# A planned order refitted: 60 zero matmuls first, zeros in every early wait, another load rate in the planner's model, and the last batch's rows stored whole

## The chip, the cores and the metric

The kernel runs on one core of a Trainium2 chip. Its time is the device time in microseconds (us) of one execution; a kernel's time is the median of several executions. The profile is of one further execution. A core has five engines that matter here: TensorE (PE, matmuls, with weight loads shown as PEld), VectorE (DVE), ScalarE (ACT), GpSimd (POOL, which issues the loads) and SyncE (SP, which issues the stores). Each engine runs its instructions strictly in the order in which the program lists them.

## The reference

Attention over 8 batches, 12 heads, 448 tokens and 64 dimensions per head, and then a feed-forward stage on the joined heads. The inputs are float32.

```python
scores = (1 / sqrt(64)) * q @ k^T                 # q, k, v: (8, 12, 448, 64)
attn   = softmax(scores);  x = attn @ v           # -> x: (3584, 768)
h      = x @ w_in                                 # w_in: (768, 2048)
g      = h * sigmoid(h)
out    = g @ w_out                                # w_out: (2048, 768) -> (3584, 768)
```

The draw has scores small enough that the kernel takes no maximum before the exp.

## The kernel before

**Units.** Heads are worked on in groups of four (`HG = 4`, so `NG = 3` groups in a batch). A unit is one group of one batch; batch 0's groups are each cut into two units of 224 queries (`PIECES`), so that there are six units for batch 0 and 21 for the others, 27 in all.

**Loads.** Keys, queries, values and both weights are loaded by POOL's queue, each cast to float16 on the way: `load_k` (tile `rk`, two buffers), `load_q` (`rq`, three), `load_v` (`V`, two), `load_w_in`, `load_w_out`. The order of the loads is written out by hand (`plan_k(0, hg)` and so on, around line 685): batch 0's keys, queries and values, then quarters of `w_in` with more queries between, batch 1's first keys, the rest of `w_in`, the first half of `w_out`, batch 1's values, the second half of `w_out`, and then batch after batch. A token of batch 0's `(i g)` layout is spread so that partition `i` of a head holds 14 tokens in a row; because of this, 32 rows of an output tile lie 14 rows apart in the output.

**Attention.** DVE turns keys and queries (`turn_k` to `KT`, `turn_q` to `QT`, lines 293 and 304). PE makes scores in bursts of one quarter of the keys (`scores`, tile `s`, line 319: two PSUM buffers of two banks), ACT takes the exp (`expo`, `E`, line 356), DVE adds up pairs of exp tiles (`add_e`, `T`, line 367), and PE makes, for each unit, the sums (part 0, with `ones`) and the two halves of the weighted values (parts 1 and 2): `attend`, tile `a`, line 383. DVE turns the sums (`sT`, line 423), inverts them (`inv`, 429), spreads them again (`rdn`, 432) and scales the values (`norm`, tile `xT`, line 440). From the second key group of batch 1 on, two units share one burst and their sums are made together.

**Feed-forward.** `ffn1` (`h`, line 454) is six matmuls for each of 16 blocks of 128 columns, followed by ACT's tanh (`th`, 465) and DVE's gate (`G` or `X`, 501). The second product is done for the first two row tiles plainly (`plain`, `o`, line 559), and for all others as quads of row tiles with seven products in place of eight (`product`, `p`, line 545); for these DVE first makes sums of the weights (`combine_w`, `D1`, `D4`, `D6` and two in `w_out_t`, line 491) and of the gated tiles (`combine_g`, `S`, line 535). Results go through ACT or DVE into `ost` and are stored by `store`, 32 rows in each DMA.

**PSUM.** `h`, `a`, `p`, `o` and the zeros' tile `z` share tag `m`: four banks in turn. So a new tile waits until the fourth one before it has been read.

**What sets the order.** Nothing is scheduled by the framework: `tc.manual_schedule` takes all engines. A planner in the kernel (`Order`, `Op`, `Ring`) runs a clock over a model of the engines at build time, with a cost for each operation (`mm`, `act`, and numbers in the `Op` calls), a rate for the loads (`DMA_RATE`, MB per us, and `DMA_TAIL`), and rings that stand for buffers. On ACT and DVE it picks, among the operations that are ready in the model, the one with the smallest ready time plus bias. On PE a burst of scores is run when it is ready and `PACE` has passed since the last, attention next, feed-forward otherwise (the loop at line 1162). The instructions are then emitted by the model's clock. On the chip the engines keep this order, whatever the real times are.

**Zeros.** Until the first `ffn1`, the planner fills a wait of PE with matmuls of a tile of zeros into `z` (`run_zeros`, line 1153):

```python
if warm["on"] and od.free["PE"] <= od.now and wait > 0.1 and od.now > 1.0:
    n = max(1, int((wait - 0.06) / mm(128)))
```

The softmax here doesn't subtract the row's maximum and nothing guards it: scores larger than these inputs give would overflow.

## Time and profile before

| | |
|---|---|
| median of five runs | 403.54 us |
| the five runs | 402.67, 403.46, 403.54, 408.07, 408.41 us |
| the profiled execution, its own time | 402.61 us |
| its span, first to last instruction | 400.8 us |
| TensorE clock granted, mean | 1.00 |
| busy: PE, DVE, ACT, POOL | 392.2, 301.2, 234.1, 88.7 us |
| loaded by POOL's queue | 22.82 MB written, in 27712 packets |
| zero matmuls | 102, 73 of them before the first score |

A line of the timeline reads: start in us from the span's start, length, engine, line of the kernel, operation, tile written <- tiles read with their shapes, number of instructions merged, and in brackets how long the engine stood idle before it and what ended that. Matmuls overlap, so that one matmul's length is more than its place in the queue; what a block costs is the distance from its first start to the next block's.

### The profile page before, as it was taken

What the parts mean: (1) busy time and instruction counts of PE and PEld (TensorE: products, weight loads), DVE (VectorE), ACT (ScalarE), POOL (GpSimd) and SP (SyncE); (2) the same over time, 40 slices, a digit from 0 to 9 for tenths busy, and PEclk for the clock granted to TensorE, in tenths of its full rate; (3) what the DMA queues carried; (4) which work ended last, traced back from release to release, by engine and by line L of the source; (5) the groups of instructions that cost most, each with busy time, mean ns of one, the idle gap of its engine ahead of it and who ended that gap; (6) DMA issues with size and microseconds to landing.
All of it is one profiled execution on the core that took longest, in us unless ns stands there. A gap on an engine that the chain in (4) does not pass through costs nothing.

```text
span 400.8 us, 9398 instructions
## 1 busy us (share of the span) xinstructions
PE 392.2 (98%) x3758; PEld 201.4 (50%) x3758; DVE 301.2 (75%) x646; ACT 234.1 (58%) x360; POOL 88.7 (22%) x160
## 2 busy tenths in 40 slices
PE   8999999999999999999999999999999999999995
PEld 7676754444444444444445444444345555555562
DVE  2566667999997987998776976986985765775763
ACT  3887886696856768467367529747776124123410
POOL 7743565623006350400170114300000000000000
PEclk9999999999999999999999999999999999999999
DMA  8999999947027942641192527411001220122014
GB/s 120 193 203 206 160 168 203 168 60 116 2 56 116 195 58 37 110 86 46 40 147 46 104 68 93 69 41 41 2 0 42 65 54 2 40 71 50 2 40 118
DMA packets 38507, 34.43 MB, mean 86 GB/s; under 512 B 11712, under 2 KB 37696, under 8 KB 38464
## 3 DMA queue, kind: packets, MB, share of 16 engines
q0 software_dynamic: 27712, 22.82, 38.9%
q1 hardware_dynamic: 10368, 10.63, 10.5%
q8 instruction: 29, 0.48, 0.5%
q10 hardware_dynamic: 384, 0.39, 0.4%
q14 instruction: 14, 0.11, 0.1%
HBM read 45.61 MB, written 11.01 MB: 141 GB/s over the span
## 4 chain that ended last, share of the span: by engine, by line
PE 95%; DVE 2%; ACT 1%; issue 1%; DVEq 0%
PE h L454 37%; PE p L545 30%; PE s L319 12%; PE a L383 12%; PE o L559 3%; PE z L1157 2%; ACT E L356 1%; DVE T L367 1%; DVE G L535 0%; DVE xT L440 0%; DVE ost L598 0%; ACT th L465 0%; DVE sT L423 0%; DVE rdn L432 0%; DVE inv L429 0%
## 5 line engine op out<-in xcount | busy, mean ns | idle before, releaser
L356 ACT ACTIVATE E<-s 128x896 f16<-128x896 f32 (+1 forms) x172 | 149.2, 915 | 46.5 <-PE s L319 45.4
L454 PE MATMUL h<-xT,w_in_t 128*128 128x448 f16 (+1 forms) x864 | 156.5, 332 | 0.2 <-DVE xT L440 0.2
L454 PEld LDWEIGHTS <-w_in_t 128*128 128x128 f16 x864 | 79.9, 98 | 70.5 <-issue 16.4
L465 ACT ACTIVATE th<-h 128x448 f16<-128x448 f32 (+1 forms) x144 | 71.6, 505 | 68.3 <-PE h L454 62.6
L501 DVE SCALAR_TENSOR_TENSOR G<-th,h 128x448 f16<-128x448 f16 (+2 forms) x144 | 75.2, 532 | 37.0 <-ACT th L465 35.5
L256 POOL DMA_DIRECT2D V<-in_v_dram x88 | 48.7, 570 | 102.6 <-PE a L383 86.0
L319 PE MATMUL s<-QT,KT 32*128 32x448 f16 (+4 forms) x864 | 54.9, 340 | 1.2 <-ACT E L356 1.2
L545 PEld LDWEIGHTS <-G 128*128 128x128 f16 x384 | 36.4, 98 | 29.1 <-issue 5.5
L545 PEld LDWEIGHTS <-S 128*128 128x128 f16 x312 | 29.1, 98 | 23.8 <-issue 5.8
L383 PE MATMUL a<-E,V 128*32 128x448 f16 (+3 forms) x864 | 40.5, 334 | 0.1
L545 PE MATMUL p<-D,G 128*128 128x384 f16 x208 | 38.0, 327 | 0.4 <-DVE xT L440 0.4
L545 PE MATMUL p<-w_out_t,S 128*128 128x384 f16 x208 | 37.0, 327 | 0.0
L440 DVE SCALAR_TENSOR_TENSOR xT<-a,rdn 128x448 f16<-128x448 f32 (+1 forms) x54 | 28.9, 562 | 8.4 <-PE a L383 7.5
L545 PE MATMUL p<-w_out_t,G 128*128 128x384 f16 x176 | 31.8, 326 | 0.0
L367 DVE TENSOR_TENSOR T<-T,E 128x1792 f16<-128x1792 f16 x20 | 21.8, 1088 | 12.8 <-ACT E L356 12.7
L319 PEld LDWEIGHTS <-KT 32*128 32x128 f16 (+2 forms) x864 | 16.4, 98 | 28.2 <-issue 27.2
L383 PEld LDWEIGHTS <-V 128*32 128x32 f16 (+2 forms) x864 | 18.4, 95 | 23.0 <-issue 15.1
L367 DVE TENSOR_TENSOR T<-E,E 128x1792 f16<-128x1792 f16 x20 | 21.7, 1083 | 6.1 <-ACT E L356 6.0
L535 DVE TENSOR_TENSOR S<-G 128x512 f16<-128x512 f16 x70 | 25.1, 415 | 0.7 <-PE p L545 0.7
L237 POOL DMA_DIRECT2D rk<-in_k_dram x24 | 13.7, 569 | 53.0 <-DVE KT L293 46.2
L293 DVE STREAM_TRANSPOSE KT<-rk 128x256 f32<-128x256 f32 (+3 forms) x48 | 16.6, 383 | 7.5 <-DMA rk<-in_k_dram 7.0
L423 DVE STREAM_TRANSPOSE sT<-a 128x448 f32<-128x448 f32 (+1 forms) x27 | 15.8, 585 | 4.7 <-PE a L383 4.3
(41 smaller groups left out, 251.1 us busy)
## 6 DMA issues: line engine op xcount, KB each, us to landing
out_dram<-ost SPq DMA_DIRECT2D x216, 48.0 KB, 1.6
rk<-in_k_dram POOLq DMA_DIRECT2D x24, 224.0 KB, 5.1
rq<-in_q_dram POOLq DMA_DIRECT2D x21, 224.0 KB, 5.7
w_out_t<-in_moe_w_out_dram POOLq DMA_DIRECT2D x8, 384.0 KB, 12.1
V<-in_v_dram POOLq DMA_DIRECT2D x43, 64.0 KB, 4.4
V<-in_v_dram POOLq DMA_DIRECT2D x40, 48.0 KB, 4.0
w_in_t<-in_moe_w_in_dram POOLq DMA_DIRECT2D x6, 256.0 KB, 7.2
w_in_t<-in_moe_w_in_dram POOLq DMA_DIRECT2D x3, 512.0 KB, 13.7
```

Of the source, the lines that this page charges most:

```text
L256: nc.gpsimd.dma_start(out=VT[b].rearrange("p h c i e -> p h c (i e)")[32 * x : 32 * (x + 1), hs, 0:count], in_=v[b, hs].rearrange("h (i g) ...
L293: nc.vector.transpose(out=turned.rearrange("p c x i -> p x c i")[:, x:y, 0:count], in_=t[:, first : first + count * (y - x)].rearrange("p ...
L319: nc.tensor.matmul(out=pS[p0 : p0 + 32 * (x1 - x0), h % 2, at : at + nq], lhsT=KT[(b, hg)][32 * h : 32 * (h + 1), c, x0:x1, :, e], rhs=QT[ ...
L356: nc.scalar.activation(out=E[(n, w)][0:kr, 2 * y : 2 * y + 2, 0:nk], in_=pS_t[(n, w, y)][0:kr, :, 0:nk], func=AF.Exp, scale=attn_scale,)
L367: nc.vector.tensor_tensor(out=T_t[n], in0=E[(n, 0)] if c == 1 else T_t[n], in1=E[(n, c)], op=ALU.add,)
L383: nc.tensor.matmul(out=a[32 * h : 32 * (h + 1), 0:nq], lhsT=w, rhs=e[k0:k1, h, at : at + nq], start=start, stop=stop,)
L440: nc.vector.scalar_tensor_tensor(out=xT[(b, cc)][:, 32 * g0 : 32 * g1], in0=acc[(n, part)][:, 0:nq], scalar=0.5, in1=rdn_t[n].rearrange("p ...
L454: nc.tensor.matmul(out=h[:, 0 : t1 - t0], lhsT=w_in_t[:, cc, 128 * f : 128 * (f + 1)], rhs=xT[(b, cc)][:, t0:t1], start=(cc == 0), stop=(c ...
L465: nc.scalar.activation(out=th, in_=h_t[(b, f, t0)][:, 0 : t1 - t0], func=AF.Tanh)
L501: nc.vector.scalar_tensor_tensor(out=dst[:, f, at + lo : at + hi], in0=th_t[(b, f, t0)][:, lo - t0 : hi - t0], scalar=1.0, in1=h_t[(b, f, ...
L535: nc.vector.tensor_tensor(out=dst[:, f0:f1], in0=x[:, f0:f1], in1=y[:, f0:f1], op=op)
L545: nc.tensor.matmul(out=pr_t[(qd, BANK[m])][:, 0:OH], lhsT=w[:, f, :], rhs=W_[m][:, f, :], start=(f == 0 and BANK[m] == m), stop=(f == HF - 1),
```

## The change

1. The planner's model: `DMA_RATE` from 0.37 to 0.405, with the loads of batch 0 counted a little heavier (1.3 and 1.25) and later keys and queries lighter (1.05 in place of 1.2); an exp's fixed cost from 0.093 to 0.052, copies' to 0.18, tanh's to 0.085; DVE's through a new `dve(n)` and 0.06 more until its result is seen; biases of tanh, gate, copies and sums; `PACE` from 3.4 to 4.2. None of these issues an instruction: they move the order of PE, ACT and DVE. The order of POOL's loads is as before.
2. Zeros: 60 at the start whatever the model says, and then in every wait over 0.05, with more of them for the same wait. The built program has 117 zero matmuls where 102 were, 62 of them before the first score.
3. Unit 0's keys are turned in two halves with its queries between, and its first scores need the first half alone.
4. Batch 7's queries are loaded head by head in another layout (four DMAs for a unit in place of one), by which 32 output rows in a row lie in 32 partitions; its results are stored with up to 128 rows in one DMA, and the last two tiles with one DMA on SP and one on ACT.
5. While batch 0's attention runs, scores that are ready go ahead of further attention parts, and an attention part goes ahead of feed-forward only when it has been ready for 0.5.

```diff
-DMA_RATE = 0.37
+DMA_RATE = 0.405
...
-def act(n):
-    return n * 0.000833 + 0.093
+def act(n, fixed=0.052):
+    return n * 0.000833 + fixed
+
+def dve(n):
+    return n / 960.0 + 0.07
...
+        if eng == "DVE":
+            tail += 0.06
...
-    PACE = 3.4
+    PACE = 4.2
...
+        if b == B - 1:
+            for h in range(HG):
+                nc.gpsimd.dma_start(
+                    out=t[32 * h : 32 * (h + 1)],
+                    in_=q[b, HG * hg + h].rearrange("(g i) d -> i g d", i=32),
+                )
+        else:
+            nc.gpsimd.dma_start(out=t, in_=group_of(q, b, hg)[:, D * g0 : D * g1])
...
-    def turn_k(b, hg):
+    def turn_k(b, hg, c0=0, c1=NCH):
...
+        last = 4 * qd + 4 == NT * B
+        w = 0
+        while w < 4:
             r, col = divmod(128 * t + 32 * w, S)
-            b = 2 * u + r
+            b, n = 2 * u + r, 1
+            cols = slice(OH * j, OH * (j + 1))
+            if b == B - 1:
+                n = 2 if last and i == j else 4 - w
+                dst = out[b * S + col : b * S + col + 32 * n, cols]
...
+            (nc.scalar if last and w else nc.sync).dma_start(
+                out=dst, in_=ost_t[(qd, i, j)][32 * w : 32 * (w + n), :]
             )
+            w += n
...
-        ld_k[(b, hg)] = od.load(1.2 * MB * TPP, lambda: load_k(b, hg), ring)
+        ld_k[(b, hg)] = od.load((1.05, 1.3)[b == 0] * MB * TPP, lambda: load_k(b, hg), ring)
...
-            mb = MB * (hg1 - hg0) * X_TOK[form(b, hg0)][x][1]
+            mb = MB * (hg1 - hg0) * X_TOK[form(b, hg0)][x][1] * (1.25 if b == 0 else 1)
...
+            if n == 0:
+                op.busy, op.emit = 0.42, lambda: turn_k(b, hg, 0, 2)
...
+        if n == 0:
+            more = Op("DVE", 0.4, lambda: turn_k(b, hg, 2, 4), [qt_op[n]], 20)
...
+    FIRST_ZEROS = 60
+    od.now = od.free["PE"]
+    od.on_pe(Op("PE", 5.0, lambda: run_zeros(FIRST_ZEROS)), "full")
+    od.now = 0.0
...
+                    if av_seq[0][0][0] < 6 and (x := qk_at()) is not None and x <= od.now + 0:
+                        break
...
-                if av is not None and av <= od.now - 0:
+                if av is not None and av <= od.now - 0.5:
...
-        if warm["on"] and od.free["PE"] <= od.now and wait > 0.1 and od.now > 1.0:
-            n = max(1, int((wait - 0.06) / mm(128)))
+        if warm["on"] and od.free["PE"] <= od.now and wait > 0.05 and od.now > 1.0:
+            n = max(1, int((wait - -0.06) / mm(128)))
```

## The prediction

> **What bounds the kernel now.** I read the page first: busy times, then the chain that ended last.

> ```profile
> span 400.8 us, 9398 instructions
> PE 392.2 (98%) x3758; PEld 201.4 (50%) x3758; DVE 301.2 (75%) x646; ACT 234.1 (58%) x360; POOL 88.7 (22%) x160
> PE 95%; DVE 2%; ACT 1%; issue 1%; DVEq 0%
> ```

> PE is busy for 98% of the span and is 95% of the chain. A change of order can gain only what PE spends on zeros, on waits, on changes of matmul shape, and at the two ends. I looked for these in the timeline, the front first.

> ```profile
> 1.03 6.06 PE L1157 MATMUL z<-zeros 128*128 128x128 f16 x73 [1.03 <-DVE zeros L214]
> 5.44 0.37 DVE L304 STREAM_TRANSPOSE QT<-rq 128x224 f32<-128x224 f32 x1
> 7.02 0.60 PE L319 MATMUL s<-QT,KT 32*128 32x224 f16 x16
> 14.36 0.57 PE L383 MATMUL a<-E,V 128*32 128x224 f16 x16
> ```

> Unit 0's queries are turned at 5.81, but PE works off zeros until 7.02. V's last quarter landed at 14.27 by the semaphore record, 0.09 before its first use. Next, PE alone:

> ```profile
> 34.05 0.37 PE L383 MATMUL a<-E,ones 96*32 96x224 f16 x6 [0.78 <-ACT E L356]
> 57.69 0.57 PE L319 MATMUL s<-QT,KT 32*128 32x448 f16 x6 [0.50 <-ACT E L356]
> 70.74 2.77 PE L559 MATMUL o<-w_out_t,G 128*128 128x384 f16 x16
> 77.39 0.57 PE L319 MATMUL s<-QT,KT 32*128 32x448 f16 x6 [0.27 <-ACT E L356]
> ```

> Waits are few. Taken as the block's start-to-start time over the shortest of its kind, they are 1.25 at 33 us, 0.33 at 36 (`h` waits for `xT`), 0.87 at 57, 0.63 at 77 and 0.51 at 122; nothing later. Last, DVE's queue around the landing of `w_out`:

> ```profile
> 60.89 0.95 DVE L491 TENSOR_TENSOR D<-w_out_t 128x1536 f16<-128x1536 f16 x1
> 63.27 1.09 DVE L367 TENSOR_TENSOR T<-T,E 128x1792 f16<-128x1792 f16 x1 [1.43 <-ACT E L356]
> 64.28 0.70 DVE L293 STREAM_TRANSPOSE KT<-rk 128x256 f32<-128x256 f32 x2
> 64.90 0.92 DVE L491 TENSOR_TENSOR D<-w_out_t 128x1536 f16<-128x1536 f16 x1
> 65.74 0.63 DVE L304 STREAM_TRANSPOSE QT<-rq 128x448 f32<-128x448 f32 x1
> 66.30 1.78 DVE L491 TENSOR_TENSOR D<-w_out_t 128x1536 f16<-128x1536 f16 x2
> 68.80 0.65 DVE L423 STREAM_TRANSPOSE sT<-a 128x448 f32<-128x448 f32 x1 [0.72 <-PE a L383]
> ```

> The loads stand close to their users: by the semaphore record `rk_2_0` landed at 63.75, `rq_9` 64.79, `rk_2_1` 67.90, `rq_10` 68.94, `rk_2_2` 71.96, `rq_11` 73.31. Here, batch 1's sums are turned (`sT` at 68.80) ahead of `KT_2_1`.

> **Front.** Zeros came 0.107 apart until 4.85 (37 of them) and 0.056 after. 62 zeros in place of 73 take 5.99 - 11 x 0.056 = 5.38, so the first score starts at 6.41, not 7.02; the turned halves of `KT` (about 0.42) and `QT` are done before that. But seven more blocks of zeros follow up to V's first use: 20, 4, 6, 2, 12, 4 and 5 (then one of 2), where six of 8, 2, 4, 7, 2, 6 stood. A block of n takes n x 0.056 + 0.11. Adding PE's blocks in the new order, without any wait: 6.41 + 0.53 + 1.23 + 0.54 + 0.33 + 0.54 + 0.44 + 0.50 + 0.27 + 0.50 + 0.50 + 0.54 + 0.78 + 0.54 + 0.33 + 0.50 + 0.39 = 14.87, against 14.36 with the same scores and sums done. The 0.61 is given back and 0.5 is lost. Unit 3's last scores, 16 together in 0.56, now stand apart at about 0.48 each: another 0.4. Bounds of the front: 0 (the zeros only fill) to +0.9; I take +0.9, since it is a plain sum of rows.

> In sentences that the rest can do without: the trace shows 37 slow zeros and then fast ones, 3.8 us after the first. [...]

> **Waits that go.** Three `h` blocks (0.58 + 0.58 + 0.67) stand between unit 5's last scores and its sums: 0.54 + 1.83 = 2.37. The sums were released 2.66 after those scores, with a tanh of 0.34 between the exps that is now queued behind them: 1.25 saved. The `h` that waited for `xT` comes later: 0.33. Unit 8's scores were 1.76 after the burst before and really ran 2.63 after it (57.69 - 55.06); the new order puts 2.9 between: 0.87. Together 2.45, less 0.9: PE leads by 1.5 when it reaches the plain products `o`, whose order does not change (bounds 0.9 and 2.4).

> **The new wait.** With faster loads in its model, the planner orders DVE so (position 95 on of the built program):

> ```
> D1, KT_2_0 x2, D1, QT_9, T_8 (second), D4, KT_2_1 x2, D4, QT_10, D6 x2, sT_7, KT_2_2 x2, inv_7, QT_11, rdn_7, sT_8, xT, inv_8, T_9, rdn_8, ...
> ```

> The POOL queue issues the same loads in the same order, each of them waiting only for landings before it, so they land when they did. DVE is in order: D1 ends about 61.5, then it stands before `KT_2_0` until 63.80 with `T_8` behind it. By spacings from the rows (KT pair 0.59, D 0.87, QT 0.53, T 1.01): D1 64.4, QT 65.3, T 65.8, D4 66.8, `KT_2_1` 67.95 (landing), D4 68.5, QT 69.4, D6 69.95 and 70.8, `sT_7` at 71.7, over by 72.3. The fourth `o` takes the PSUM bank that `sT_7` empties (four buffers of tag m in turn): it starts at 72.4. PE would have been there at 70.74 - 1.5 = 69.2. So 3.2 of waiting, and PE is 1.7 behind before. Next late: `QT_11` stands before `rdn_7` until 73.36; then rdn 0.56, sT 0.56, xT 0.53, inv 0.15, T 1.01, rdn 0.56, D 0.87 and three xT at 0.53 bring the last `xT` of batch 1 to 79.8. The sixth matmul of `h_1_0` needs it; `h_1_8` starts at 80.05. Before, `h_1_0`, `h_1_8` and `s_10` were done at 79.04; now at 80.05 + 1.23 + 0.51 = 81.8: behind by 2.75. The 0.63 at 77 is covered by this.

> **Behind it.** No two bursts of scores after 81 are closer than 2.54, so the 0.51 at 122 goes; five are at 2.54, which 2.63 would make 0.45 of waiting at most. From the first `h` of batch 1 on, changes from `h`, `p`, `o` to `s` or `a` fall from 72 to 68, at 0.095 each (`h` 1.231 against 1.135): 0.38. Behind by 1.9 when PE ends, at 397.8.

> **Queries and stores of batch 7.** Twelve loads in place of three: 9 x 0.57 of POOL. They were issued 31, 24 and 28 us before DVE used them (221.17 to 252.83, 241.87 to 266.18, 253.75 to 281.75), and that hides even four times their 5.4 us; without that cover each would cost its 5 us. [...] The end:

> ```profile
> 383.45 14.89 SPq L593 DMA_DIRECT2D out_dram<-ost  x24
> 395.95 0.56 DVE L598 TENSOR_TENSOR ost<-p,s 128x384 f32<-128x384 f32 x1 [0.26 <-PE p L545]
> ```

> DVE ends at 396.51, but the last two of SP's 24 issues start at 397.54 and 397.90 and land about 399.56; 1.27 of closing follow. Now one issue of 64 rows on SP and one on ACT follow at once: 0.05 + 1.65, perhaps 0.2 more for size, + 1.27 = 3.15 in place of 4.32. I take -1.0 (bounds -1.5 and +0.3, were a large store much slower).

> **What costs nothing.** The second half of unit 0's `KT` is two more DVE instructions of about 0.13 to 0.26; they run between 5.8 and 6.2, where DVE idled for 2.18 until 7.99, and serve scores that start at 8.2; without that gap they would add their 0.4 to the next `KT`. The refitted durations, biases and PACE issue nothing themselves; they act through the order, which is counted above.

> **Sum.** Against the execution's own 402.61 (span 400.83): +1.9 - 1.0 = +0.9, so 403.5. The median of the five runs lies 0.93 above that execution: 404.4.

> **Rivals.** First: the loads land earlier than in this one execution, or DVE's detour is covered, and the order works as planned. For it: one more us of lead for the loads already frees most of the 3.2. Against: DMA moves 190 to 210 GB/s here and was late in all of this stage. Then 1.5 + 0.9 + 1.0 = 3.4 less: 400.1. Second, slower: the loads are late by L. Before, `s_9` started 0.98 after its `QT` was done, so it loses L - 1; now nothing is left and all behind it moves by L. From L = 3.2, 5% of the time until 67.9, it passes 407.6; with 4, 408.4. For it: the runs shown reach 408.41; against: three of five lie within 0.9. Third, no effect at all of `FIRST_ZEROS`: it is in the sum already, with the wrong sign.

> **How the numbers follow.** Forecast 0.66, first rival 0.18, second 0.16. Half of the first lies under 399.5 (faster by over 1%, about what a measurement of this kernel tells from no change), three quarters of the second over 407.6: faster 0.09, same 0.79, slower 0.12. The forecast's own terms give 402 to 406; the range, with most of both rivals, 400.2 to 407.6.

> **What would show it.** Right: the first score at 6.4; no PE wait at 33 or 57; `KT` of batch 2 ends DVE's longest wait near 64; the fourth `o` starts after 72 behind a wait for `sT`, and an `h` waits for `xT` near 78 to 80; SP's last issue within 0.1 of DVE's end. Wrong: the fourth `o` at 69 to 70, or waits of PE after 90 over 1 us in all.

## The result, and the profile after

The new kernel takes 402.85 us (median of 54 executions, 401.24 to 405.88) where the kernel before takes 403.50 (94 executions beside it, 402.53 to 408.93). The ratio is 0.9969, interval 0.9956 to 0.9983. It is a little faster, by 0.65 in the medians, where the prediction had it 0.9 slower.

In some executions TensorE's clock is granted at one half for some microseconds (0.50 from 15.3 to 22.1 us in the trace of `before_b`), and the ratios take most of these in, so that below medians are compared, and "undisturbed" means a mean clock of 0.997 or more: 403.41 for the kernel before (71 of 126 executions beside the experiments), 402.77 for the new one (53 of 66). Such cuts of the clock are part of the result: 46 of those 126 had a mean clock of 0.992 or less and took 405.7 to 409.6 us, and one of the 66.

The profiled execution of the new kernel is one of its longest, 404.24 us. From the page, the span, TensorE's busy time and the chain that ended last:

```profile
span 402.5 us, 9430 instructions
PE 392.3 (97%) x3773; PEld 203.2 (50%) x3773; DVE 299.5 (74%) x647; ACT 235.2 (58%) x360; POOL 94.5 (23%) x169
PE 79%; DMA 15%; POOL 3%; DVE 1%; issue 1%; POOLq 0%
```

The chain was 95% PE before and had no loads in it. Now 15% of it are loads and 3% POOL: the end hangs on landings. The timeline of PE (start, length, line, tiles, number of matmuls, idle time before and what ended it):

```profile
1.03 6.21 PE L1193 MATMUL z<-zeros 128*128 128x128 f16 x62 [1.03 <-DVE zeros L220]
7.17 0.58 PE L336 MATMUL s<-QT,KT 32*128 32x224 f16 x16
15.37 0.57 PE L400 MATMUL a<-E,V 128*32 128x224 f16 x16
72.04 2.76 PE L576 MATMUL o<-w_out_t,G 128*128 128x384 f16 x16 [2.30 <-DVE sT L440]
75.76 1.63 PE L400 MATMUL a<-E,V 128*32 128x448 f16 x32 [0.96 <-DVE sT L440]
79.82 2.02 PE L471 MATMUL h<-xT,w_in_t 128*128 128x448 f16 x9 [1.24 <-DVE xT L457]
```

There is no wait at 33, 57 or 77 us any more and none after 80; three new ones stand at 72, 76 and 80, together 4.50. DVE's timeline, some of its rows, shows why:

```profile
60.35 0.96 DVE L508 TENSOR_TENSOR D<-w_out_t 128x1536 f16<-128x1536 f16 x1 [0.27 <-DMA w_out_t<-in_moe_w_out_dram]
63.48 0.70 DVE L310 STREAM_TRANSPOSE KT<-rk 128x256 f32<-128x256 f32 x2 [2.17 <-DMA rk<-in_k_dram]
67.62 0.70 DVE L310 STREAM_TRANSPOSE KT<-rk 128x192 f32<-128x192 f32 x2 [0.21 <-DMA rk<-in_k_dram]
71.35 0.64 DVE L440 STREAM_TRANSPOSE sT<-a 128x448 f32<-128x448 f32 x1
72.86 0.70 DVE L310 STREAM_TRANSPOSE KT<-rk 128x256 f32<-128x256 f32 x2 [0.88 <-DMA rk<-in_k_dram]
74.01 0.65 DVE L321 STREAM_TRANSPOSE QT<-rq 128x448 f32<-128x448 f32 x1 [0.32 <-DMA rq<-in_q_dram]
78.62 1.68 DVE L457 SCALAR_TENSOR_TENSOR xT<-a,rdn 128x448 f16<-128x448 f32 x3
```

It stands 2.17 for `rk_2_0` (landed at 63.45) with a queue of ready work behind it, and `sT_7`, which frees the PSUM bank of the fourth `o`, comes at 71.35. Its last stand is 0.32 for `rq_11` (landed at 73.99); from there its rows follow one another without a gap up to the three `xT` for which `h` waits at 79.82. The end of the timeline:

```profile
385.79 13.55 SPq L615 DMA_DIRECT2D out_dram<-ost  x12
398.06 1.38 ACTq L615 DMA_DIRECT2D out_dram<-ost  x2
398.29 0.56 DVE L621 TENSOR_TENSOR ost<-p,s 128x384 f32<-128x384 f32 x1 [0.26 <-PE p L562]
```

Twelve issues on SP in place of 24. From DVE's last end (398.84) to the end of the span are 3.63 us, where 4.33 were before.

### The profile page after: what moved, and what is told of

It reads as the page before. It is cut to its first block, busy times and chain, and to the rows that moved or that the text cites. A ratio compares the mean times of both kernels' runs of the same rounds, so it can differ in the third digit from the quotient of the medians.

```text
span 402.5 us, 9430 instructions
## 1 busy us (share of the span) xinstructions
PE 392.3 (97%) x3773; PEld 203.2 (50%) x3773; DVE 299.5 (74%) x647; ACT 235.2 (58%) x360; POOL 94.5 (23%) x169
## 4 chain that ended last, share of the span: by engine, by line
PE 79%; DMA 15%; POOL 3%; DVE 1%; issue 1%; POOLq 0%
PE h L471 32%; PE p L562 30%; PE a L400 9%; PE s L336 8%; DMA rq<-in_q_dram 7%; DMA w_in_t<-in_moe_w_in_dram 5%; DMA V<-in_v_dram 2%; POOL V L270 1%; POOL rk L243 1%; POOL w_out_t L288 0%; DVE xT L457 0%; POOL rq L257 0%; DVE rdn L449 0%; DVE T L384 0%; DVE w_out_t L508 0%
## 5 line engine op out<-in xcount | busy, mean ns | idle before, releaser
L518 DVE SCALAR_TENSOR_TENSOR G<-th,h 128x448 f16<-128x448 f16 (+2 forms) x144 | 74.5, 532 | 36.6 <-ACT th L482 35.1
L552 DVE TENSOR_TENSOR S<-G 128x512 f16<-128x512 f16 x70 | 26.4, 418 | 3.8 <-PE p L562 3.7
L310 DVE STREAM_TRANSPOSE KT<-rk 128x192 f32<-128x192 f32 (+3 forms) x49 | 16.8, 379 | 9.7 <-DMA rk<-in_k_dram 9.5
L562 PE MATMUL p<-D,S 128*128 128x384 f16 x104 | 19.1, 327 | 0.0
```

Of the source, the lines that this page charges most:

```text
L518: nc.vector.scalar_tensor_tensor(out=dst[:, f, at + lo : at + hi], in0=th_t[(b, f, t0)][:, lo - t0 : hi - t0], scalar=1.0, in1=h_t[(b, f, ...
L552: nc.vector.tensor_tensor(out=dst[:, f0:f1], in0=x[:, f0:f1], in1=y[:, f0:f1], op=op)
L562: nc.tensor.matmul(out=pr_t[(qd, BANK[m])][:, 0:OH], lhsT=w[:, f, :], rhs=W_[m][:, f, :], start=(f == 0 and BANK[m] == m), stop=(f == HF - 1),
```

## The experiments

### Does the new load model cost, and where?

My theory was the prediction's own mechanism: with faster loads in its model the planner queues the turns of batch 2's keys ahead of `sT_7`, DVE stands at landings, and the end follows them; the gain comes from elsewhere. The rivals: loads that are queued for sooner are the gain itself; or the gain is only the tail.

**`after_again`: the new kernel once more, for a second trace.**

> The new kernel unchanged, for a second trace and for the base of the comparisons sent with it. Theory A (the new order stands at loads that land late: PE's three waits at 72, 76 and 80 us, 2.30 + 0.96 + 1.24 = 4.50, follow the landing of batch 2's keys): ratio to before 0.995 to 0.999; in the trace each of these waits again follows a landing (rk_2_0, rk_2_2, rq_11), and when those land x us earlier than the 63.45, 72.84 and 73.99 of the first trace, PE's last matmul starts about x earlier than its 397.92, less or more by the front. Theory B (the front decides: how many of the 60 zeros are slow): if they run slow for 5.5 us again, first score near 7.2 as in the first trace, if for 3.8 us as in the kernel before, near 6.4, and the end moves by the same 0.8.

Median 402.78, ratio 0.9971 (0.9935 to 1.0007). Its trace (own time 403.10) repeats the waits, all earlier:

```profile
62.38 0.70 DVE L310 STREAM_TRANSPOSE KT<-rk 128x256 f32<-128x256 f32 x2 [2.00 <-DMA rk<-in_k_dram]
71.03 2.76 PE L576 MATMUL o<-w_out_t,G 128*128 128x384 f16 x16 [2.19 <-DVE sT L440]
72.86 0.65 DVE L321 STREAM_TRANSPOSE QT<-rq 128x448 f32<-128x448 f32 x1 [0.35 <-DMA rq<-in_q_dram]
78.67 2.02 PE L471 MATMUL h<-xT,w_in_t 128*128 128x448 f16 x9 [1.24 <-DVE xT L457]
```

`rk_2_0` landed 1.09 sooner (62.36), `rq_11` 1.16 sooner (72.83), and PE's last matmul starts 1.14 sooner (396.78). In both traces the fourth `o` starts 8.6 behind the landing of `rk_2_0` (72.04 - 63.45 = 8.59; 71.03 - 62.36 = 8.67), and the `h` that waits last 5.8 behind that of `rq_11` (79.82 - 73.99 = 5.83; 78.67 - 72.83 = 5.84). Two traces can't tell which landing counts, though the chain that ended last runs over `rq_11` in the first; `after_p29` and `e_z0` below tell. The first score started at 6.11, 1.06 sooner too, with 28 slow zeros in place of 50, so this pair does not tell the front from a landing either.

**`b_rate`: the kernel before with the new load model alone.**

```diff
-DMA_RATE = 0.37
+DMA_RATE = 0.405
-        ld_k[(b, hg)] = od.load(1.2 * MB * TPP, lambda: load_k(b, hg), ring)
+        ld_k[(b, hg)] = od.load((1.05, 1.3)[b == 0] * MB * TPP, lambda: load_k(b, hg), ring)
...
```

> The kernel before with nothing but the new model of the loads (DMA_RATE 0.405, batch 0 heavier, later keys and queries lighter). DVE's order is then D1, KT_2_0, T_8, QT_9, D4, T_8, KT_2_1, QT_10, KT_2_2, D6, QT_11, sT_7: the sums of unit 7 stand behind the landings of rk_2_2 (71.96 in the trace of before) and rq_11 (73.31). Theory A: sT_7 starts at 73.4 to 74.5 in place of 68.80, the fourth plain product at 74 to 75.5 in place of 70.74, and the end comes 3 to 4.5 later: 406.5 to 408, ratio 1.008 to 1.011. Theory B (queued for sooner gains): faster than before, 0.995 to 0.999. Theory C: 1.000 within 0.001.

406.48 against 403.84 beside it: 2.6 slower (2.7 by the undisturbed), at the lower edge of the forecast; ratio 1.0038 (1.0001 to 1.0076). The lines of DVE and PE:

```profile
72.53 0.65 DVE L304 STREAM_TRANSPOSE QT<-rq 128x448 f32<-128x448 f32 x1 [0.36 <-DMA rq<-in_q_dram]
73.09 0.61 DVE L423 STREAM_TRANSPOSE sT<-a 128x448 f32<-128x448 f32 x1
73.75 2.76 PE L559 MATMUL o<-w_out_t,G 128*128 128x384 f16 x16 [0.68 <-DVE sT L423]
```

`sT_7` comes right behind the turn of `rq_11`, and the fourth `o` 3.0 later than before. The wait ahead of it is only 0.68 since this execution was late already (first `o` at 60.46, 2.3 later than before). The refit alone costs; the rival that it is the gain falls.

**`e_rate`: the new kernel with the old load model.**

```diff
-DMA_RATE = 0.405
+DMA_RATE = 0.37
-        ld_k[(b, hg)] = od.load((1.05, 1.3)[b == 0] * MB * TPP, lambda: load_k(b, hg), ring)
+        ld_k[(b, hg)] = od.load(1.2 * MB * TPP, lambda: load_k(b, hg), ring)
...
```

> The new kernel with the old model of the loads (DMA_RATE 0.37, keys and queries at 1.2, values at 1) and everything else new. DVE's order is then D1, KT_2_0, D4, QT_9, D4, sT_7, D6, inv_7, KT_2_1, rdn_7, sT_8: the sums of unit 7 are turned before the wait for rk_2_1, not after it. Theory A (the refit of the loads costs; the rest gains): DVE stands to about 63.8 for KT_2_0, then 0.59 + 0.87 + 0.53 + 0.87 bring sT_7 to 66.7 and over by 67.3 in place of 71.9; the fourth plain product starts at 67 to 68.5, not 72.04, and of the 4.50 of waits 2 to 3.5 go: 2 to 3.5 us faster than the new kernel, ratio to before 0.988 to 0.992. Theory B (loads queued for sooner are where the gain comes from): the gain over before is lost, ratio 1.000 or more. Theory C (the gain is the tail or the zeros, and the order of DVE is covered): the same as the new kernel within 0.4 us, 0.996 to 0.998.

402.02, ratio 0.992 (0.9885 to 0.9955): faster than the new kernel, but by 0.8 and not by 2 to 3.5. The three waits are gone, and others have come before them on PE:

```profile
37.12 0.55 PE L471 MATMUL h<-xT,w_in_t 128*128 128x224 f16 x2 [0.77 <-DVE xT L457]
52.84 1.31 PE L471 MATMUL h<-xT,w_in_t 128*128 128x224 f16 x12 [0.32 <-DVE G L518]
59.45 0.37 PE L336 MATMUL s<-QT,KT 32*128 32x448 f16 x2 [0.32 <-ACT E L373]
60.26 0.57 PE L336 MATMUL s<-QT,KT 32*128 32x448 f16 x6 [0.44 <-ACT E L373]
```

With 0.23 at 55.76 they make 2.08. So the old rate does not only move the keys: it changes PE's order from 15 us on. Taking all of the refit back mixes two things, and the next kernel separates them.

**`t_k25`: one number, the weight of batch 2's keys in the model.**

```diff
-        ld_k[(b, hg)] = od.load((1.05, 1.3)[b == 0] * MB * TPP, lambda: load_k(b, hg), ring)
+        ld_k[(b, hg)] = od.load((1.05, 1.3, 1.05, 2.5)[(b == 0) + 3 * (b == 2)] * MB * TPP, lambda: load_k(b, hg), ring)
```

> The new kernel with one number changed: the planner counts batch 2's keys 2.5 times as heavy, so that their turns are queued later, and all before 60 us stays as it is. DVE's order is then D1, D4, KT_2_0, T_8, QT_9, D4, D6, D6, KT_2_1, sT_7, QT_10, inv_7, rdn_7, sT_8, and KT_2_2 and QT_11 behind the first xT. Theory A: DVE works off three sums of weights before it stands for keys, and sT_7 starts near 69.5 to 70 in place of 71.35; PE's waits at 72, 76 and 80 us (4.50 and 4.26 in the two traces of the new kernel) shrink to 1.5 to 2.5: 2 to 2.7 us faster than the new kernel, median 400 to 400.8, ratio 0.989 to 0.992. Theory B (loads queued for sooner are the gain): slower than the new kernel. Theory C (the landings pin the stage, whatever the order): the same within 0.5.

400.14, ratio 0.9891 (0.9831 to 0.9951). DVE and PE of its trace:

```profile
68.64 0.61 DVE L440 STREAM_TRANSPOSE sT<-a 128x448 f32<-128x448 f32 x1
69.30 2.76 PE L576 MATMUL o<-w_out_t,G 128*128 128x384 f16 x16
75.65 2.01 PE L471 MATMUL h<-xT,w_in_t 128*128 128x448 f16 x9 [0.84 <-DVE xT L457]
```

The loads land as ever (`rk_2_0` at 62.57), but DVE does its weight sums first, the fourth `o` does not wait, and 0.84 is left of the 4.50 and 4.26 of the new kernel's two traces. The median is 2.7 below the new kernel's, less than the 3.4 to 3.7 of waits that went. This is the version that beats both. Repeated:

> The new kernel with batch 2's keys counted 2.5 times as heavy and all 117 zeros, repeated. Theory A (the zeros of the front keep the clock, the later turns of the keys spare the long wait): 0 or 1 of the executions at a mean clock of 0.993 or less, median 399.8 to 400.6, ratio 0.987 to 0.992. Theory B (with the wait for the keys gone, cuts of the clock show at the end as they do in the kernel before): a third of the executions at 403 or more.

399.87, ratio 0.9868 (0.98 to 0.9937), with the clock cut in one execution of six (406.27). Of both runs' twelve executions two had a clock of 0.986 or less; the median of all is 400.05.

### Why did the added 0.93 not come?

**`before_b`, `before_c`: the kernel before, unchanged, twice.**

> The kernel before, unchanged, for a second trace of it. Its profiled execution (402.61) is among its shortest; with the clock granted at 0.998 or more its executions have a median of 403.6. Theory A (that execution was lucky in its front or in its loads, and a usual one waits about 1 us more): 403.1 to 404.3, and PE shows one more wait, or a longer one, between 15 and 80 us, so that its last matmul starts near 396.6 and not at 395.58. Theory B (the difference lies outside the span, in what comes before and after it): span again 400.8 with PE's last start at 395.6, and a larger distance from the span to the time.

> The same once more: of two further traces at least one should lie near the usual 403.6, and the three together say which waits vary. A clock granted below 1 in some stretch is to be expected in one execution of three; where it falls is what this looks for.

`before_c` took 403.18: 44 slow zeros in place of 35, first score at 7.48 in place of 7.02, V landed at 14.70 in place of 14.27, PE's last start at 396.17 in place of 395.58. From the first score on it is the same execution (388.69 against 388.56). So the 0.57 between these two was made in the front, and not by a further wait, as I had expected. `before_b` took 405.93 and holds a cut of the clock. PE's timeline, and then the table by stretches (length, PE busy and its matmuls, granted clock, DMA share, GB/s):

```profile
15.01 0.71 PE L383 MATMUL a<-E,V 128*32 128x224 f16 x16 [0.64 <-DMA V<-in_v_dram]
```

```profile
14.00:16.00 2.00, 1.36 (x28) 0.83 1.24 198
16.00:18.00 2.00, 2.00 (x40) 0.50 1.23 199
...
20.00:22.00 2.00, 2.00 (x37) 0.50 1.21 189
```

Half the clock for 6.8 us: 3.3 later at the first `o` (61.51 against 58.19), and 3.33 at the end. In both traces this kernel paid all that happened in the front.

**`before_p29`, `after_p29`: 29 more zeros at the very start, unknown to the planner, in both kernels.**

```diff
             warm["z"] = ps.tile([128, 512], FP32, name="z", tag="m", bufs=4)
+            n += 29
```

> The kernel before with 29 zeros more in its first block of zeros, of which the planner knows nothing: the order of everything else is unchanged. 29 x 0.056 = 1.62. Theory A (this kernel waits for its own engines, hardly for loads, so that a late front is paid in full; only V's landing, at 14.3 to 14.9 in its traces against a first use at 14.36, can cover some of it): 1.1 to 1.6 slower than the kernel before, ratio 1.0025 to 1.004. Theory B (late fronts are taken up everywhere by the waits for loads near 60 us): the same within 0.3.

> The new kernel with the same 29 zeros more, again unknown to its planner. Theory A (the fourth plain product starts 8.6 behind the landing of rk_2_0, whatever happened before): PE reaches it 1.62 later and waits that much less, 0.6 to 0.7 in place of 2.30 and 2.19; the end moves by 0 to 0.5, median 402.7 to 403.3, ratio 0.997 to 0.9985. Theory B (the lead that PE has built up is what the new kernel gains by): 1.2 to 1.6 slower, 404 to 404.4.

29 x 0.056 = 1.6 of delay. The kernel before: 405.99 beside 403.73, 2.3 slower, more than the delay (its trace adds 0.88 and 0.50 at 22 and 28 us, in which PE stands for nothing that the profile shows). The new kernel: 402.81, no change at all. Its wait takes the delay up:

```profile
71.29 2.76 PE L576 MATMUL o<-w_out_t,G 128*128 128x384 f16 x16 [0.64 <-DVE sT L440]
78.28 2.01 PE L471 MATMUL h<-xT,w_in_t 128*128 128x448 f16 x9 [1.24 <-DVE xT L457]
```

The 0.64 is as forecast, but by luck: the fourth `o` starts 9.40 behind `rk_2_0` (61.89), not 8.6, for here DVE hardly waits for these keys and stands 1.01 for `rq_10` (68.30). What holds in all is the last landing. DVE stands for `rq_11` (0.53, to 72.45), and `h` again starts 5.83 behind it with the same wait of 1.24. So the front of the new kernel costs nothing within such bounds, and what its end hangs on is the landing of `rq_11`.

**`e_z0`: the 60 zeros at the start left to the planner's own filling** (91 before the first score).

```diff
-    FIRST_ZEROS = 60
-    od.now = od.free["PE"]
-    od.on_pe(Op("PE", 5.0, lambda: run_zeros(FIRST_ZEROS)), "full")
-    od.now = 0.0
```

> The new kernel without the 60 zeros at the start: the planner fills up to the first score by its model, which makes 91 zeros before the first score in place of 62 and 146 in all in place of 117. Theory A (the front is paid back at the loads: DVE stands for rk_2_0 whatever PE does): the first score starts 29 x 0.056 = 1.6 later, near 8.0, but the fourth plain product starts again about 8.6 us behind rk_2_0's landing, and the end moves by less than 0.5. Theory B (the zeros at the front set the end): 1.2 to 1.6 slower than the new kernel, ratio to before 1.000 or above.

403.16, 0.4 over the new kernel (0.1 by the undisturbed), ratio 0.9959 (0.9923 to 0.9995). The fixed count of 60 is worth little, for the same reason. In its trace the fourth `o` starts 9.25 behind `rk_2_0` and not 8.6, since DVE stands for `rq_10`; the `h` that waits last starts 5.84 behind `rq_11`.

### The stores

**`e_tail`: batch 7's queries and stores as before.** `load_q`, `plan_q` and `store` of the kernel before, all else new.

> The new kernel with the old load of batch 7's queries and the old stores of 32 rows each. Theory A: only the end changes. From DVE's last instruction to the span's end the trace of before had 4.33 and that of the new kernel 3.63: 0.7 slower than the new kernel, at most 1.0. Theory C (the tail is the whole gain): 1.2 slower, ratio to before 1.000. Were the large stores or the twelve loads a burden on the other loads: 0.3 or less slower.

403.05, 0.3 over the new kernel and not 0.7. Its trace has 3.82 between DVE's end and the span's end: of the 0.7 that the new kernel gains at the end, 0.5 goes with the new order of the last products (SP's last issue starts 1.0 behind DVE's end in place of 1.4), and 0.2 with the large stores. This trace also has a cut of the clock, 0.50 from 72 to 75 us, behind a wait of 2.37; the fourth `o` took 4.3 in place of 2.8, the waits at 75 and 79 vanished, and the end did not move: PE's last matmul starts 323.9 behind `rq_11`, as in the two traces of the new kernel.

### The zeros and the clock

**`b_vz`: the kernel before with 8 zeros ahead of the first product with V, unknown to the planner.**

```diff
         lone = len(ns) == 1
+        if part == 1 and ns[0] == 0:
+            run_zeros(8)
```

> The kernel before with 8 zeros more, put right ahead of the first product with V, where PE waits for V's landing in some executions (0.64 in the trace with the clock at 0.992); the planner knows nothing of them and the order is unchanged. Theory A (a wait for V in a stage where PE does little is what halves the clock): 0 or 1 of 12 executions with a mean clock of 0.992 or less, where the kernel before has 26 of 77; the others take 403.5 to 404.0, since 8 x 0.056 = 0.45 lies in the wait or is paid. Theory B (the clock is cut for another reason): 3 to 5 of 12 at 0.992 or less again.

403.55 in the median, and all 12 executions lie between 402.80 and 403.95 at a clock of 0.997 or more, where 9 of 23 beside them, and 46 of 126 in all, were at 0.992 or less. At the latter rate 12 without one have a chance of 0.4%. Eight zeros in that one wait keep the clock of the kernel before. It is not these zeros alone that do: in `before_p29`, where PE comes 1.6 later and V has landed, all 12 executions are at 0.996 or more too. And a wait there need not cost the clock: in the trace of `e_rate` PE stands 0.83 for V without zeros, and none of its 12 executions is at 0.992 or less. That the new kernel's zeros, 5 of which stand at this place, earn something is likely by this, but not shown.

**`e_zf`: the new kernel with the old rule for zeros behind the first 60.**

```diff
-        if warm["on"] and od.free["PE"] <= od.now and wait > 0.05 and od.now > 1.0:
-            n = max(1, int((wait - -0.06) / mm(128)))
+        if warm["on"] and od.free["PE"] <= od.now and wait > 0.1 and od.now > 1.0:
+            n = max(1, int((wait - 0.06) / mm(128)))
```

> The new kernel with the old rule for zeros behind the first 60 (waits over 0.1, fewer for the same wait): 86 zeros in place of 117. Theory A (more zeros in the front keep the clock; the landing of rk_2_0 sets the end): a median within 0.3 of the new kernel's 402.8, but 2 to 4 of 12 executions with a clock of 0.992 or less. Theory B (the zeros do nothing, the new order is what keeps the clock): a median within 0.3 and at most 1 of 12 at 0.992 or less. Theory C (the zeros cost 0.9, as the prediction summed, and their loss is seen at the end): 402.0 or less.

405.55, 2.7 slower, with 7 of 12 executions at 0.993 or less. But it is no clean test: with less time in zeros the planner also moved the turn of `rk_2_2` ahead of `sT_7`, and the trace has a wait of 3.13 ahead of the fourth `o`. The next kernels ask which of the two costs the clock.

**`e_zf_p18`, `e_zf_b`, `e_zf_c`, and `t_k25_zf` twice.** The first is `e_zf` with `n += 18` added to the first block, as above; the second and third repeat `e_zf`; the last is `t_k25` with the edit of `e_zf`.

> The new kernel with the old rule for zeros behind the first block (86 in all), and 18 more in that first block, of which the planner knows nothing: PE comes 18 x 0.056 = 1.0 later to everything, with the same thin blocks behind. Theory A (the long wait of PE halves the clock): the wait ahead of the fourth plain product falls from 3.13 to about 2.1, as in the new kernel; 0 to 2 of 12 executions at a clock of 0.993 or less, median 402.6 to 403.3. Theory B (the thin front halves it): 5 to 8 of 12 again, median 405 or more.

> The new kernel with the old rule for zeros, once more, for a trace with the clock cut: in two of three executions. Theory A: it falls to one half behind the wait ahead of the fourth plain product, from about 72 us on. Theory B: it falls between 12 and 25 us, as in the kernel before's trace with the cut (15.4 to 22).

> The same once more, should the other show no cut of the clock: theory A has it from about 72 us on, theory B between 12 and 25 us.

> The new kernel with batch 2's keys counted 2.5 times as heavy, and with the zeros behind the first 60 by the old rule (waits over 0.1, fewer for the same wait): 86 zeros where that kernel has 117. With the wait for the keys largely gone, this shows what the zeros cost. Theory A (the later blocks of zeros cost 0.5 to 0.9 at the front, as the prediction summed): 0.3 to 0.9 faster than with all 117, median 399.3 to 399.9. Theory B (they only fill waits for V and for the exps that are there anyway): the same within 0.3. Theory C (they keep PE's clock up): slower, by 0.5 or more, and more zeros or scores 0.1 apart in the front.

> The thin front with the keys turned later, beside e_zf_p18 on the same chip. Theory A (the long wait): again no execution, or one, at 0.993 or less, median 399.9 to 400.5. Theory B (the thin front): a third or more of them, some at 402 to 405.

`e_zf_p18`: 404.06, one of 12 at 0.991 and seven at 0.994 or 0.995; the wait in its trace is 3.98 and not 2.1, since `rk_2_2` landed late (72.65) and `sT_7` stood behind it. `e_zf_b` (404.96) and `e_zf_c` (404.05) both show the cut, behind that wait. The timeline and the stretches of the former:

```profile
73.65 4.44 PE L576 MATMUL o<-w_out_t,G 128*128 128x384 f16 x16 [4.50 <-DVE sT L440]
```

```profile
74.00:76.00 2.00, 2.00 (x9) 0.58 0.78 139
76.00:78.00 2.00, 2.00 (x8) 0.56 0.01 2
```

`t_k25_zf` took 400.22 with none of six below 0.997. `t_k25_zf_b` had the same program at 398.89 to 402.15 in four executions and at 406.29 to 408.11, with a clock of 0.973 to 0.975, in four. Its trace is one of the latter, by stretches:

```profile
14.00:16.00 2.00, 1.82 (x28) 0.53 1.25 200
16.00:24.00 8.00, 8.00 (x116) 0.50 1.21 197
24.00:32.00 8.00, 8.00 (x112) 0.50 1.13 211
```

So both theories were half right. A long wait at 72 can be followed by one short cut of 3.4 us (in four traces; not in those of `after`, `after_again` and `e_zf`, with waits of 2.30, 2.19 and 3.13), and a thin front in some executions by a long one, here some 20 us. The 31 zeros cost nothing that can be measured (undisturbed medians of 400.2 without them and 400.0 with them, ten executions each), and such executions were 4 of 14 without them, 2 of 12 with them: too few to say by these runs alone that they guard the clock. What shows that the front decides over the clock is `b_vz`, with `before_p29`.

## Why the prediction was wrong, step by step

**Front.** The first score came at 7.17 and 6.11, not 6.41: the number of slow zeros, 37 in the prediction (35 are over 0.1 apart, as counted here), was 50 and 28. From the first score to the first `o` the new kernel gained 1.1 (49.96 and 50.12 against 51.17); the prediction's terms made it 1.5 - 0.61 = 0.9. Size nearly right, and without effect, as `after_p29` shows.

**Waits that go.** 33, 36, 57 and 122 us: gone, as forecast.

**The new wait.** Right in place and kind, and in the first two traces in time: the forecast had `sT_7` at 71.7 and the fourth `o` at 72.4 for a landing at 63.75, 8.65 behind it; it starts 8.6 behind. What sets the end is the second part of that chain, from `QT_11` to the last `xT`, and it was right as well: `h_1_0`, `h_1_8` and `s_10` were to be done 81.8 - 73.31 = 8.5 behind the landing of `rq_11`, and are 82.28 - 73.99 = 8.3 behind it. `h` waits for `xT` from its fourth matmul on, at 79.82 (forecast: the sixth, with `h_1_8` at 80.05). The 0.96 at 76, for the bank that `sT_8` empties, was not named but lies on the same way.

**Behind it.** Forecast 0.51 + 0.38 = 0.89 given back behind 81 us. Behind by 82.28 - 79.04 = 3.24 there and by 397.92 - 395.58 = 2.34 at the end: 0.90.

**Tail.** Mis-sized: -0.7, not -1.0. The last stores issue at once, as said, but the last 96 KB took 2.48 from the start of the issue to landing on ACT's queue (398.88 to 401.36) and 2.23 on SP's, where I had 1.65 and 0.2 for size. The loads of batch 7's queries were covered, as said: the four of a unit were in 5.7 to 6.9 us after the first was issued, where the one load of a unit took 4.1 to 5.4 in the trace of before.

**The steps that failed are two: "so they land when they did", and the last, "the median of the five runs lies 0.93 above that execution".** The sum prices the wait with the landings of one trace, `rq_11` at 73.31. Taken as a distance from that landing it was right: it had 403.5 - 73.31 = 330.2, and the traces' own times lie 330.25, 330.27, 330.44 and 330.56 behind `rq_11` (`after`, `after_again`, `after_p29`, `e_z0`); that PE's part came out 0.24 short and the tail's 0.3 long, so that the two cancel, is luck. But the landing itself moves: `rq_11` came between 72.45 and 73.99 in the five traces with the new kernel's order, 72.83 in the median, 0.48 sooner than assumed. And I took the distance of one execution from the median as a constant of the chip. It is a property of the kernel before, which pays its front in full: later V, more slow zeros, a cut clock. The new kernel takes such delays up in the very waits that I had found. Without the 0.93 and the 0.48, 404.4 becomes 403.0, against 402.85. The rest would ask for `rq_11` at 72.6 in the timed executions, where it was not measured.

**Rivals.** The first (loads land sooner, 400.1) had the right direction and the wrong law: `rq_11` 1.16 sooner moves the end by 1.14 and leaves the last wait in place (1.24); 400.05 was reached only by taking the order away (`t_k25`). The second has the same law from the other side; no undisturbed trace has loads so late. The third, no effect of `FIRST_ZEROS`, was dismissed as counted already and came close: `e_z0` is 0.1 to 0.4 slower.

**What stays open.** Which part of the change keeps the clock in the new kernel is shown only for the kernel before (`b_vz`); its order differs too. For why some executions of one program lose the clock and others do not there is only an estimate below, by a count over the traces; no run set out to test it.

## What to carry to other kernels

An engine that is in order and stands at a landing ties the end to that landing, as DVE did here (`rq_11` landed 1.16 sooner in `after_again` than in `after`, and PE's last matmul started 1.14 sooner): price such a wait with the landings of several executions, and do not add the spread of a kernel that had no such wait. When a planner's model is refitted, look for the one place where ready work is queued behind a load: a heavier weight for those loads alone gained 2.7 us here, where taking the whole refit back gained 0.8. Where PE waits for a load early on, a few zeros in that wait may keep the clock and cost little (`b_vz`: 403.55, where undisturbed executions of the kernel before take 403.41).

## What the runs showed of the hardware

What the cuts have in common, by a count of mine, is little work ahead of them. The end of the slow zeros and the start of each cut are a whole number of 3.413 us apart (5.07 and 15.30 in `before_b`, three lengths; 6.72 and 71.58 in `e_tail`, nineteen). So I divided the 20 traces into stretches of 3.413 from the end of the slow zeros on, and counted the work in each in zero matmuls (128 columns through the whole array, others by their columns and share of the array; at 0.056 us each, a stretch holds 61). Of 2272 stretches outside a cut seven held 21.6 or less, and six of these were followed by a cut, all six that there are; the seventh, with 20.6 in `b_rate`, was not. None of the others, from 23.0 on, was; the thinnest in `before` and `after` held 24.4 and 24.5. Within the cuts, the clock stayed at one half after stretches with 20.1 or less and came back after those with 24.1 or more. `b_vz` agrees: the stretch from 13.98 to 17.39 of its trace holds 28.9, eight of them the added zeros. The slow zeros ended at 3.7 to 7.1 us, so that by this division the same thin work can lie in one stretch in one execution and be shared by two in another. As an explanation of the cuts this is an estimate: the count was made after the fact, with modelled ends of matmuls, and no run set out to test it.

Slow zeros at the start (0.107 apart in `before` and `after`, where those behind them are 0.056 apart) numbered 24 to 55 over the 20 traces (28 and 50 in the two of the new kernel), and the same load, `rk_2_0`, landed between 61.52 and 63.75 us, `rq_11` between 71.70 and 73.99 where the clock was not cut ahead of it.
